# First token group of an mLSTM cell with a SwiGLU block: dense landing of k and q, 64-row turns, values in column halves, and another order of loads and weight conversion

## The chip, the core and the metric

The kernel runs on one core of a Trainium2 chip. The metric is the time of one execution on the device in microseconds (us), lower is better; the runs' median is compared. The engines are TensorE (PE, matrix products and transposes), VectorE (DVE), ScalarE (ACT, also table functions), GpSimd (POOL) and SyncE (SP, which here only asks for DMA transfers). Each engine runs its own instructions in program order and waits on semaphores for the others. On-chip memory has 128 partitions; matrix products write to PSUM banks.

## What is computed

The reference, cut to what matters (B=4, H=8, S=768, D=40; 3072 tokens, model width 320, hidden width 1536):

```python
for t in range(S):                                  # mLSTM cell, per batch and head
    m_new = max(f[t] + m, i[t])
    f_stab, i_stab = exp(f[t] + m - m_new), exp(i[t] - m_new)
    C = f_stab * C + i_stab * outer(v[t], k[t])
    n = f_stab * n + i_stab * k[t]
    y[t] = sigmoid(o[t]) * (C @ q[t]) / max(abs(n @ q[t]), 1.0)
x = y.transpose(0, 2, 1, 3).reshape(B * S, H * D)
out = (silu(x @ w_gate) * (x @ w_val)) @ w_out      # weights come as float64
```

## The kernel before

**Stages.** The sequence is cut into six groups of 128 tokens; each group has 4 batches x 128 tokens = 512 columns. Within a group the cell is computed with products over the 128 tokens and a carried state. Then comes the feed-forward block: twelve hidden blocks m of 128 features (`hidden(0, m)` in the first group) and the output product (`project_all`). Group 0 has a prologue of its own (L526 to L664), in which nothing of the feed-forward block can run yet. The order of instructions is written out by hand: the calls in the prologue, then for each hidden block m the lists `ahead` (which weight blocks are converted behind it) and `slots` (what else is emitted behind it, L978 onward).

**The prologue.** P is a pair of batches (16 heads), u one batch. Seven burn products (L521) start PE. The masked decay weights are summed in eight PSUM banks (wps: L532, L536, L541) and exponentiated by ACT (`first_exp`, L547) into W0, which lives in h_sb[:, 0:8]. k and q are transposed (`first_turn`, L561) from tiles in which each head has 64 columns, 40 of data and 24 of zeros; `first_scores` (L571) multiplies, DVE applies the weights (L575). `first_own(u)` (L582) multiplies W0 with the values, eight heads, 128x128 by 128x41. `first_x(u)` (L587 to L590) divides, `first_gate(P)` (L596) multiplies with the sigmoid of the output gate (`sig`, L515) and POOL repeats 64 columns as padding (L597). `first_seam(P)` (L616) transposes x into xT, and `first_state(P)` (L604) makes the carried state. The first `hidden` product, gv_ps (L706), needs xT of both pairs and the converted weights of block 0.

**Weights.** They come as 64-bit floats and are converted on the chip: `scale(j)` is two ACT products (L212, L214), `join(j)` two DVE instructions (L221, L222), `rounded(j)` one addition on DVE or POOL (L229). They are loaded in pieces (`piece_load`, L187): p0 and p1 hold one hidden block each (m = 0, 1), p2 to p6 two each (p2: m = 2, 3). A piece has a gate part (partitions 0 to 63, asked for by SP) and two value parts (partitions 64 to 127, asked for by ACT up to p4). p2 lands in h_sb[:, 1:6], which W0 occupies first, p3 in h_sb[:, 8:13], p4 in wo_sb, the others in two buffers of their own.

**Later gates.** f_sb and i_sb hold the gates of the later 640 tokens. Their sums (`late_sums`, L296 to L298) and running maxima (`late_maxima`, L301 to L303) are written to M_dram and read back as w_sb for group 1 (L484), which first goes into `add` (L379).

**hidden(0, m)** makes two products into two PSUM banks (four such banks rotate), then ACT takes silu of the first (L711) and DVE multiplies with the second (L712). Block m+2 therefore needs the banks that L711 and L712 of block m release.

Of the kernel before, what the change touches and what calls it, by code (L numbers as in the profile page):

```python
# [18 lines left out]
L = 128  # L19
# [5 lines left out]
def kernel(  # L25
# [47 lines left out]
    def flat(t):  # L73
        return t.rearrange("p c t -> p (c t)")

    def bank(name, tag="cell"):
        return psum.tile([128, 512], F32, name=name, tag=tag)
# [26 lines left out]
    def heads(P):  # L104
        return slice(P * UH, (P + 1) * UH)
# [31 lines left out]
    def load(dst, a, c, P):  # L137
        nc.sync.dma_start(out=dst[:, heads(P), 0:D], in_=tokens(a, c, P))

    def copy(eng, dst, src):  # L140
        if eng is nc.scalar:
            nc.scalar.copy(dst, src)
        else:
            eng.tensor_copy(dst, src)

    def gate_rows(a):
        return a.rearrange("b h s -> (b h) s")
# [3 lines left out]

    nc.scalar.dma_start(out=f0, in_=spread_rows(f_gate))
    nc.sync.dma_start(out=i0, in_=spread_rows(i_gate))
    nc.scalar.dma_start(out=flat(f_sb), in_=gate_rows(f_gate)[:, L:])
    nc.scalar.dma_start(out=flat(i_sb), in_=gate_rows(i_gate)[:, L:])


    raws = {}
    PIECES = [("gv", 0, 1), ("gv", 1, 1)] + [("gv", m, 2) for m in range(2, NFC, 2)] + [("o", m, 4) for m in range(0, NFC, 4)]

    def piece_load(p, home=None):
        kind, m, n = PIECES[p]
        if kind == "gv":
            a, d = NKC, n * 128
            gate_w, val_w = (w[:, m * 128:(m + n) * 128].rearrange("(c p) f -> p c f", p=HP) for w in (moe_w_gate, moe_w_val))
            src = [(slice(0, HP), slice(0, NKC), gate_w), (slice(HP, 128), slice(0, NKC - 1), val_w[:, 1:]),
                   (slice(HP, 128), slice(NKC - 1, NKC), val_w[:, 0:1])]
            queues = (nc.sync,) + 2 * (nc.scalar if p < 5 else nc.sync,)
        else:
            a, d = n, DM  # L170
            src = [(slice(0, 128), slice(0, n), moe_w_out[m * 128:(m + n) * 128].rearrange("(a p) d -> p a d", p=128))]
            queues = (nc.sync,)
        if src[0][2].dtype == F32:
            for r, cs, w in src:
                if kind == "o":
                    nc.sync.dma_start(out=wo_sb[r, m:m + n, :], in_=w)
                else:
                    for x in range(n):
                        nc.sync.dma_start(out=wgv_sb[r, m + x, cs], in_=w[:, :, ts(x, 128)])
            return  # L180
        if home is None:
            raw = conv.tile([128, 4 * NKC * 128], U32, name="raw")
        else:
            raw = home.rearrange("p a t -> p (a t)").bitcast(U32)
        raw = raw[:, 0:2 * a * d]
        for (r, cs, w), queue in zip(src, queues):
            queue.dma_start(out=raw[r].rearrange("p (a d) -> p a d", a=a)[:, cs], in_=w.bitcast(U32))  # L187
        words = raw.rearrange("p (a d two) -> p a d two", two=2, a=a)
        raws[p] = (words[:, :, :, 0], words[:, :, :, 1])
        split(p)  # L190
# [40 lines left out]
    def convert(j, eng=None):  # L231
        scale(j)
        join(j)
        rounded(j, eng)

    for P in range(2):
        load(k_sb, k, 0, P)
        load(q_sb, q, 0, P)
        load(v_sb, v, 0, P)
    load(o_sb, o_gate, 0, 0)  # L240


    junk = early.tile([128, 512], BF16)
# [51 lines left out]
    def late_sums():  # L295
        nc.vector.tensor_tensor_scan(flat(f_sb), flat(keep1), flat(f_sb), 0.0, op0=ALU.mult, op1=ALU.add)  # L296
        nc.gpsimd.memset(step1, 0.0)
        nc.gpsimd.tensor_sub(i_sb, i_sb, f_sb)  # L298
# [166 lines left out]
    def xT(n):  # L465
        return xT_sb
# [47 lines left out]
    def sig(P):  # L514
        nc.scalar.activation(o_sb[:, heads(P)], o_sb[:, heads(P)], AF.Sigmoid)  # L515


    def burn(n, tag="cell"):
        t = bank("burn", tag)
        for _ in range(n):  # L520
            nc.tensor.matmul(t, lhsT=junk[:, 0:128], rhs=junk, start=True, stop=True)  # L521
# [22 lines left out]
    def first_exp(P):  # L544
        for j in range(2):
            for u in (2 * P, 2 * P + 1):
                nc.scalar.activation(W0[:, u * H + j * HH:u * H + (j + 1) * HH], wps[u, j], AF.Exp)  # L547

    w_end = early.tile([128, BH, 1], F32)

    def first_values(P):
        nc.gpsimd.tensor_copy(w_end[:, heads(P)], W0[:, heads(P), end])
        nc.gpsimd.tensor_tensor(vw_sb[:, heads(P)], v_sb[:, heads(P)], w_end[:, heads(P)].to_broadcast([128, UH, D1]),
                                op=ALU.mult)

    def first_turn(P, src, dst, engs):
        for b in range(2):
            tp = bank("tp_kq").rearrange("p (a t) -> p a t", t=L)
            for a in range(UA // 2):
                h = P * UH + b * H + 2 * a  # L560
                nc.tensor.transpose(tp[:, a, :], src[:, h:h + 2, :].rearrange("p h d -> p (h d)"), ident)  # L561
            a = P * UA + b * UA // 2
            copy(engs[b], dst[:, a:a + UA // 2, :], tp)

    def first_scores(P):
        for b in range(2):
            sp = [bank("sp").rearrange("p (a t) -> p a t", t=L) for _ in range(2)]
            a0 = P * UA + b * UA // 2
            for a in range(UA // 2):
                for two in range(2):  # L570
                    nc.tensor.matmul(sp[two][:, a, :], lhsT=kT[half(two), a0 + a, :], rhs=qT[half(two), a0 + a, :],  # L571
                                     start=True, stop=True)
            W = W0[:, 2 * a0:2 * a0 + H].rearrange("p (a two) t -> p two a t", two=2)
            for two in range(2):
                nc.vector.tensor_tensor(W[:, two], sp[two], W[:, two], op=ALU.mult)  # L575
# [3 lines left out]
    def first_own(u):  # L579
        first_y[u] = bank("first_y", "gen")[:, 0:H * D1].rearrange("p (h d) -> p h d", d=D1)  # L580
        for h in range(H):
            nc.tensor.matmul(first_y[u][:, h, :], lhsT=W0[:, u * H + h, :], rhs=v_sb[:, u * H + h, :], start=True, stop=True)  # L582

    def first_x(u):
        y = first_y.pop(u)
# [4 lines left out]
        nc.vector.tensor_tensor(x_sb[:, u, 0:DM].rearrange("p (h d) -> p h d", d=D), y[:, :, 0:D],  # L590
                                den.to_broadcast([128, H, D]), op=ALU.mult)

    def first_gate(P):
        for u in (2 * P, 2 * P + 1):
            x = x_sb[:, u, 0:DM].rearrange("p (h d) -> p h d", d=D)
            nc.vector.tensor_tensor(x, x, o_sb[:, u * H:(u + 1) * H], op=ALU.mult)  # L596
        nc.gpsimd.tensor_copy(x_sb[:, 2 * P:2 * P + 2, DM:], x_sb[:, 2 * P:2 * P + 2, 0:HP])  # L597

    def first_state(P, tag="cell"):
        ps = small("add", tag=tag)  # L600
# [6 lines left out]
    def first_kept(P, ps, eng):  # L607
        copy(eng, state(2)[:, P * UA:(P + 1) * UA], ps)

    def first_seam(P, engs):  # L610
        for c, eng in zip(range(0, NKC, 2), engs):
            cs = range(c, min(c + 2, NKC))
            tp = bank("tp_x")[:, 0:len(cs) * 2 * L].rearrange("p (c u s) -> p c u s", u=2, s=L)
            for w in cs:
                for b in range(2):
                    nc.tensor.transpose(tp[:, w - c, b, :], x_sb[:, 2 * P + b, ds(w * HP, 2 * HP)], ident)  # L616
            copy(eng, xT(0)[:, c:c + len(cs), 2 * P * L:(2 * P + 2) * L].rearrange("p c (u s) -> p c u s", u=2), tp)

    burn(7)
    banks = [(u, j) for j in range(2) for u in range(B)]  # L620
    for f in (first_mask, first_inputs, first_maxima):
        for u, j in banks:
            f(u, j)
    first_exp(0)
    first_turn(0, k_sb, kT, (V, V))
    first_turn(0, q_sb, qT, (A, V))
    first_exp(1)
    first_values(0)
    first_scores(0)
    first_own(0)  # L630
    late_sums()
    first_turn(1, k_sb, kT, (A, A))
    first_x(0)
    first_turn(1, q_sb, qT, (A, V))
    load(o_sb, o_gate, 0, 1)
    piece_load(0)
    first_own(1)
    first_values(1)
    first_scores(1)
    first_x(1)  # L640
    sig(0)
    piece_load(1)
    burn(3)
    first_own(2)
    piece_load(2, h_sb[:, 1:1 + NKC])
    sig(1)
    burn(2)
    first_own(3)
    first_gate(0)
    first_x(2)  # L650
    first_x(3)
    first_gate(1)
    first_seam(0, (A, A, V))
    scale(0)
    ps1 = first_state(1, "gen")
    burn(1, "gen")
    piece_load(3, h_sb[:, NH - NKC:])
    join(0)
    first_seam(1, (A, A, V))
    rounded(0, V)  # L660
    first_kept(0, first_state(0), A)
    first_kept(1, ps1, V)
    convert(1, V)
    nc.scalar.activation(warm, warm, AF.Silu)  # L664
    piece_load(4, wo_sb)
    piece_load(5)


    pair = early.tile([BH, PP], F32)
# [289 lines left out]
    def load_all(dst, a, n):  # L959
        for P in range(2):  # L960
# [7 lines left out]
    ahead[0] = []  # L968
    ahead.update({4: [6], 5: [7, 8], 6: [9], 7: [10], 8: [11], 9: [], 10: [], 11: []})
    slots = {  # L970
        0: [run(convert, 2, V), run(late_maxima), run(load_all, k_sb, k, 1),
            run(nc.sync.dma_start, out=M_dram, in_=flat(M_sb)), run(load_all, q_sb, q, 1)],
        1: [run(piece_load, 6), run(late_decay)],
        2: [run(nc.scalar.activation, step1, step1, AF.Exp), run(decay_rows), run(weights_load, 1), run(load_all, v_sb, v, 1)],
        3: [run(late_turns)],
        4: [run(decay), run(cap_table)],
# [131 lines left out]
```

## Time and profile before

| what | us |
|---|---|
| median of 3 runs | 512.71 (512.23 to 512.75) |
| profiled execution, its own time | 513.3 |
| span in its trace | 511.5 |
| PE busy, share of the span | 505.1, 99% |
| end of the first pair's exponentials (ACT L547) | 11.61 |
| first scores product on PE (L571) | 12.52 |
| end of the last score product on DVE (L575) | 24.07 |
| end of the second gate (L596) | 28.96 |
| first gv_ps product (L706) | 31.92 |
| p2: parts asked for (ACT, SP, ACT) | 24.67, 24.92, 26.27 |
| p2: last part landed | 36.40 |
| scaling of block 2 on ACT (L212) | 36.98 |
| first gv_ps product of block 2 | about 40.66 |

Times in the trace run from the start of the span; the profiled execution is 1.8 us longer than its span. A timeline line reads: start, length, engine, line, operation, output<-inputs, shape, count, and in brackets the idle time before it with what ended it. "SPq" and "ACTq" lines are requests for transfers; the landing is a later event. In the DMA view, q1 is the queue that SP's requests go to and q10 that of ACT's.

### The profile page before, as it was taken

Reading aid. Unit: us, or ns where it says so; the run is one execution under the profiler, and the core shown is the slowest. Engines: PE = TensorE matmul, PEld = TensorE weight load, DVE = VectorE, ACT = ScalarE, POOL = GpSimd, SP = SyncE. Lnnn points to the kernel's source line nnn. Section 1 sums busy time; section 2 is a strip of 40 time slices with the busy share of each in tenths; the row PEclk is TensorE's granted clock in tenths of the full one; section 3 lists DMA queues with packets and bytes.
Section 4 is the critical chain, followed back from the end, with each engine's and each line's share of the span. In section 5 each row is a group of like instructions: output and inputs, shape, how many; then the busy total and the mean of one; then the engine's idle time right before and its main releaser. Section 6 shows DMA issues by size and latency. Waiting matters only on the chain.

```text
span 511.5 us, 14788 instructions
## 1 busy us (share of the span) xinstructions
PE 505.1 (99%) x6307; PEld 428.8 (84%) x6309; DVE 332.3 (65%) x539; ACT 204.8 (40%) x394; POOL 255.0 (50%) x274
## 2 busy tenths in 40 slices
PE   8999999999999999999999999999999999999997
PEld 4964445667888899988899888899988899988896
DVE  5779767887897777687466678467658554233421
ACT  3477655448512339312339321338421340223210
POOL 1303427475879663367652457652447650166710
PEclk9999999999999999999999999999999999999999
DMA  9999999698502992501993411993101200000001
GB/s 123 174 232 238 168 194 244 148 177 119 88 1 45 143 130 39 92 3 26 156 134 42 75 21 27 156 131 43 42 3 19 37 3 27 27 1 0 1 14 38
DMA packets 205497, 43.27 MB, mean 85 GB/s; under 512 B 193432, under 2 KB 200600, under 8 KB 205432
## 3 DMA queue, kind: packets, MB, share of 16 engines
q1 hardware_dynamic: 203444, 39.49, 49.4%
q10 hardware_dynamic: 1988, 2.85, 2.4%
q8 instruction: 49, 0.80, 0.7%
q14 instruction: 16, 0.13, 0.1%
HBM read 35.68 MB, written 4.01 MB: 78 GB/s over the span
## 4 chain that ended last, share of the span: by engine, by line
PE 91%; DMA 2%; DVE 2%; issue 1%; POOL 1%; ACT 1%; SPq 0%; DVEq 0%; ACTq 0%; POOLq 0%
PE gv_x L854 26%; PE o_ps L777 23%; PE gv_y L854 21%; PE gv_ps L706 5%; PE o_ps L723 5%; DMA w_sb<-M_dram 2%; PE inter L402 2%; PE intra L411 2%; PE sp L353 2%; PE first_y L582 1%; PE add L379 1%; POOL w_sb L493 1%; PE burn L521 1%; PE tp_kq L561 1%; PE sp L571 1%
## 5 line engine op out<-in xcount | busy, mean ns | idle before, releaser
L854 PE MATMUL gv_x<-xT,wgv_sb 64*128 64x256 f32 x720 | 89.1, 377 | 0.0
L854 PEld LDWEIGHTS gv_x<-xT,wgv_sb 64*128 64x128 f32 x720 | 69.6, 187 | 7.9 <-issue 0.2
L777 PE MATMUL o_ps<-wo_sb,h_sb 128*128 128x160 f32 x480 | 67.4, 300 | 0.0
L777 PEld LDWEIGHTS o_ps<-wo_sb,h_sb 128*128 128x128 f32 x480 | 65.6, 190 | 1.7 <-issue 1.7
L902 ACT ACTIVATE h_sb<-gv_x 128x256 f32<-128x256 f32 x30 | 11.5, 383 | 117.8 <-PE gv_x L854 117.8
L706 PE MATMUL gv_ps<-xT,wgv_sb 64*128 64x512 f32 x240 | 53.7, 596 | 0.3 <-DVE wgv_sb L229 0.3
L706 PEld LDWEIGHTS gv_ps<-xT,wgv_sb 64*128 64x128 f32 x240 | 23.6, 187 | 24.4 <-issue 23.2
L854 PE MATMUL gv_y<-q_sb,wgv_sb 64*128 64x256 f32 x360 | 44.0, 377 | 0.0
L854 PE MATMUL gv_y<-xT,wgv_sb 64*128 64x256 f32 x360 | 43.9, 376 | 0.0
L854 PEld LDWEIGHTS gv_y<-q_sb,wgv_sb 64*128 64x128 f32 x360 | 34.9, 187 | 4.2 <-DVE tmp L894 0.4
L854 PEld LDWEIGHTS gv_y<-xT,wgv_sb 64*128 64x128 f32 x360 | 35.0, 187 | 3.9
L364 POOL TENSOR_TENSOR vw_sb<-v_sb,w_sb 128x656 f32<-128x656 f32 x10 | 14.6, 1467 | 41.2 <-ACT w_sb L509 40.0
L777 PE MATMUL o_ps<-wT,S 128*128 128x160 f32 x240 | 33.4, 299 | 0.0
L777 PEld LDWEIGHTS o_ps<-wT,S 128*128 128x128 f32 x240 | 32.9, 190 | 0.0
L509 ACT ACTIVATE w_sb<-w_sb,g_T 128x64 f32<-128x64 f32 x128 | 31.0, 334 | 0.0
L854 PE MATMUL gv_x<-q_sb,sw 64*128 64x256 f32 x240 | 31.0, 376 | 0.0
L875 POOL TENSOR_TENSOR h_sb<-x_sb 128x512 f32<-128x512 f32 x12 | 15.8, 1314 | 24.6 <-ACT x_sb L874 24.6
L895 POOL TENSOR_TENSOR tmp<-tmp 128x512 f32<-128x512 f32 x15 | 20.0, 1332 | 14.5 <-DVE tmp L894 14.5
L875 POOL TENSOR_TENSOR h_sb<-tmp 128x512 f32<-128x512 f32 x13 | 16.5, 1269 | 21.5 <-ACT tmp L874 21.5
L744 POOL TENSOR_TENSOR S<-h_sb 128x256 f32<-128x256 f32 x30 | 22.6, 752 | 9.2 <-DVE h_sb L875 7.3
L854 PE MATMUL gv_y<-q_sb,sw 64*128 64x256 f32 x200 | 27.0, 388 | 0.0
L723 PE MATMUL o_ps<-wo_sb,h_sb 128*128 128x320 f32 x96 | 26.9, 437 | 0.0
(221 smaller groups left out, 984.6 us busy)
## 6 DMA issues: line engine op xcount, KB each, us to landing
w_sb<-M_dram SPq DMA_DIRECT2D x10, 512.0 KB, 7.1
k_sb<-in_k_dram SPq DMA_DIRECT2D x12, 320.0 KB, 7.4
v_sb<-in_v_dram SPq DMA_DIRECT2D x12, 320.0 KB, 5.5
o_sb<-in_o_gate_dram SPq DMA_DIRECT2D x12, 320.0 KB, 6.8
raw<-in_moe_w_out_dram SPq DMA_DIRECT2D x3, 1280.0 KB, 7.5
x_sq<-k_sb SPq DMA_DIRECT2D x64, 40.0 KB, 2.0
q_sb<-in_q_dram SPq DMA_DIRECT2D x32, 64.0 KB, 3.8
out_dram<-tmp SPq DMA_DIRECT2D x24, 80.0 KB, 1.7
```

Source lines behind the costliest of these rows:

```text
L353: nc.tensor.matmul(sp[two][half(i), a, :], lhsT=kT[feats(two), P * UA + a, half(i)], rhs=qT[feats(two), P * UA + a, half(i)], start=True, ...
L364: eng.tensor_tensor(vw_sb[:, heads(P)], v_sb[:, heads(P)], w_sb[:, heads(P), last].to_broadcast([128, UH, D1]), op=ALU.mult)
L402: nc.tensor.matmul(inter[two][half(i), a, :], lhsT=qT[feats(two), P * UA + a, half(i)], rhs=state(2 * n + i)[feats(two), P * UA + a, :], s ...
L509: nc.scalar.activation(w_sb[:, h], w_sb[:, h], AF.Exp, bias=g_T[:, n, h:h + 1], scale=-1.0)
L706: nc.tensor.matmul(ps[i], lhsT=wgv_sb[half(i), m, kc, :], rhs=x[half(i), kc, :], start=(kc == 0), stop=(kc == NKC - 1))
L723: nc.tensor.matmul(ps[u], lhsT=hid(g, m)[:, ts(u, L)], rhs=wo_sb[:, m, :], start=(m == 0), stop=(m == NFC - 1))
L744: eng.tensor_tensor(S1[:, k], lo[:, second_half], hi[:, second_half], op=ALU.add)
L777: nc.tensor.matmul(node[x][:, i], lhsT=lhs(k)[:, ts(i, L)], rhs=rhs(k), start=start and k == 0 and i == 0, stop=stop and k == KH - 1, skip ...
L854: nc.tensor.matmul(ps[:, i, cols], lhsT=lhs(c)[half(i)], rhs=rhs(c)[half(i)], start=start and c == 0, stop=stop and c == n - 1, skip_group ...
L875: (nc.vector if k == KH - 1 else nc.gpsimd).tensor_tensor(h_sb[:, 2 * k + 1], uw[:, 0], uw[:, 1], op=ALU.mult)
L895: nc.gpsimd.tensor_tensor(uw[:, :, second_half], uw[:, :, second_half], uw[:, :, first_half], op=ALU.add)
L902: nc.scalar.activation(h[:, first_half], x[:, 0, first_half], AF.Silu)
```

## The change

- k and q of the first group land dense (16 heads x 40 columns) in h_sb[:, 8:13], q first; DVE (q of pair 0) and POOL (the other three) copy them into the padded tiles. v follows.
- The requests for f_sb and i_sb move from ACT's start to SP, right behind p2's gate part.
- k and q are turned by `turn_one`, which transposes 64 rows at a time into two banks, and x by `seam`, likewise; `first_turn` and `first_seam` go.
- `first_own` is split into column halves: each head's product becomes two of 64 output rows.
- The prologue's order is written anew: own(0) and own(1) both come before scores(1), state(0) before own(3). Pair 0's gate and its padding are on POOL, pair 1's padding on ACT, rounding of block 0 on POOL. Three groups of burn products (3, 2 and 1) go.
- p1's value parts are asked for by POOL. p2 is asked for in two steps: the gate part and the first value part behind the second gate, the second value part behind the second seam's copies; the first value part stands on ACT behind the padding. SP's requests for p3's and p4's gate parts come directly behind the late gates; the value parts of p4 stand behind block 0's silu on ACT.
- The conversion of block 2 and the sums of the later gates come before hidden(0, 0) instead of behind it, so on ACT the scaling of block 2 precedes block 0's silu, and on DVE its joining, its rounding and the scan of the sums precede block 0's product. The running maxima, the M_dram write and the load of the next q come one block later.

`piece_load` gets an argument `parts` (which of the three transfers to ask for); the rest of it is unchanged.

```diff
@@ -151,39 +151,45 @@
 
     nc.scalar.dma_start(out=f0, in_=spread_rows(f_gate))
     nc.sync.dma_start(out=i0, in_=spread_rows(i_gate))
-    nc.scalar.dma_start(out=flat(f_sb), in_=gate_rows(f_gate)[:, L:])
-    nc.scalar.dma_start(out=flat(i_sb), in_=gate_rows(i_gate)[:, L:])
+
+    def late_gates():
+        nc.sync.dma_start(out=flat(f_sb), in_=gate_rows(f_gate)[:, L:])
+        nc.sync.dma_start(out=flat(i_sb), in_=gate_rows(i_gate)[:, L:])
...
+    homes = {}
+
-            queues = (nc.sync,) + 2 * (nc.scalar if p < 5 else nc.sync,)
+            queues = (nc.sync,) + 2 * (nc.gpsimd if p == 1 else nc.scalar if p < 5 else nc.sync,)
...
+        if p in homes:
+            raw = homes[p]
+        elif home is None:
             raw = conv.tile([128, 4 * NKC * 128], U32, name="raw")
         else:
             raw = home.rearrange("p a t -> p (a t)").bitcast(U32)
-        raw = raw[:, 0:2 * a * d]
-        for (r, cs, w), queue in zip(src, queues):
+        raw = homes[p] = raw[:, 0:2 * a * d]
+        for (r, cs, w), queue in [(src[x], queues[x]) for x in parts if x < len(src)]:
             queue.dma_start(out=raw[r].rearrange("p (a d) -> p a d", a=a)[:, cs], in_=w.bitcast(U32))
...
+    dense = h_sb[:, NH - NKC:].rearrange("p m t -> p (m t)").rearrange("p (x h d) -> p x h d", x=4, d=D)
+
+    def load_dense(x, a, P):
+        nc.sync.dma_start(out=dense[:, x], in_=tokens(a, 0, P))
+
+    def spread(eng, x, dst, P):
+        copy(eng, dst[:, heads(P), 0:D], dense[:, x])
+
     for P in range(2):
-        load(k_sb, k, 0, P)
-        load(q_sb, q, 0, P)
+        load_dense(2 * P, q, P)
+        load_dense(2 * P + 1, k, P)
+    for P in range(2):
         load(v_sb, v, 0, P)
-    load(o_sb, o_gate, 0, 0)
 
 
...
+    def first_ends(P):
+        nc.gpsimd.tensor_copy(w_end[:, heads(P)], W0[:, heads(P), end])
+
     def first_values(P):
-        nc.gpsimd.tensor_copy(w_end[:, heads(P)], W0[:, heads(P), end])
         nc.gpsimd.tensor_tensor(vw_sb[:, heads(P)], v_sb[:, heads(P)], w_end[:, heads(P)].to_broadcast([128, UH, D1]),
                                 op=ALU.mult)
-
-    def first_turn(P, src, dst, engs):
-        for b in range(2):
-            tp = bank("tp_kq").rearrange("p (a t) -> p a t", t=L)
-            for a in range(UA // 2):
-                h = P * UH + b * H + 2 * a
-                nc.tensor.transpose(tp[:, a, :], src[:, h:h + 2, :].rearrange("p h d -> p (h d)"), ident)
-            a = P * UA + b * UA // 2
-            copy(engs[b], dst[:, a:a + UA // 2, :], tp)
 
...
     def first_own(u):
         first_y[u] = bank("first_y", "gen")[:, 0:H * D1].rearrange("p (h d) -> p h d", d=D1)
         for h in range(H):
-            nc.tensor.matmul(first_y[u][:, h, :], lhsT=W0[:, u * H + h, :], rhs=v_sb[:, u * H + h, :], start=True, stop=True)
+            for i in range(2):
+                nc.tensor.matmul(first_y[u][half(i), h, :], lhsT=W0[:, u * H + h, half(i)], rhs=v_sb[:, u * H + h, :],
+                                 start=True, stop=True)
 
...
-    def first_gate(P):
-        for u in (2 * P, 2 * P + 1):
+    def first_gate(P, engs, pad):
+        for u, eng in zip((2 * P, 2 * P + 1), engs):
             x = x_sb[:, u, 0:DM].rearrange("p (h d) -> p h d", d=D)
-            nc.vector.tensor_tensor(x, x, o_sb[:, u * H:(u + 1) * H], op=ALU.mult)
-        nc.gpsimd.tensor_copy(x_sb[:, 2 * P:2 * P + 2, DM:], x_sb[:, 2 * P:2 * P + 2, 0:HP])
+            eng.tensor_tensor(x, x, o_sb[:, u * H:(u + 1) * H], op=ALU.mult)
+        copy(pad, x_sb[:, 2 * P:2 * P + 2, DM:], x_sb[:, 2 * P:2 * P + 2, 0:HP])
 
...
-    def first_seam(P, engs):
-        for c, eng in zip(range(0, NKC, 2), engs):
-            cs = range(c, min(c + 2, NKC))
-            tp = bank("tp_x")[:, 0:len(cs) * 2 * L].rearrange("p (c u s) -> p c u s", u=2, s=L)
-            for w in cs:
-                for b in range(2):
-                    nc.tensor.transpose(tp[:, w - c, b, :], x_sb[:, 2 * P + b, ds(w * HP, 2 * HP)], ident)
-            copy(eng, xT(0)[:, c:c + len(cs), 2 * P * L:(2 * P + 2) * L].rearrange("p c (u s) -> p c u s", u=2), tp)
-
+    spread(V, 0, q_sb, 0)
+    spread(G, 1, k_sb, 0)
     first_exp(0)
-    first_turn(0, k_sb, kT, (V, V))
-    first_turn(0, q_sb, qT, (A, V))
+    turn_one(0, q_sb, qT, (V, A))
+    turn_one(0, k_sb, kT, (V, A))
     first_exp(1)
+    first_ends(0)
+    spread(G, 2, q_sb, 1)
+    spread(G, 3, k_sb, 1)
+    first_scores(0)
+    turn_one(1, q_sb, qT, (A, A))
+    turn_one(1, k_sb, kT, (A, A))
     first_values(0)
-    first_scores(0)
+    piece_load(0)
+    load(o_sb, o_gate, 0, 0)
+    load(o_sb, o_gate, 0, 1)
     first_own(0)
+    first_ends(1)
+    first_values(1)
+    first_own(1)
+    first_x(0)
+    first_x(1)
+    first_scores(1)
+    sig(0)
+    first_gate(0, (G, G), G)
+    scale(0)
+    first_own(2)
+    first_x(2)
+    sig(1)
+    ps0 = first_state(0)
+    first_own(3)
+    piece_load(1)
+    seam(0, 0, (A, A, A, A))
+    first_x(3)
+    first_gate(1, (V, V), A)
+    join(0)
+    piece_load(2, h_sb[:, 1:1 + NKC], (0, 1))
+    rounded(0)
+    ps1 = first_state(1, "gen")
+    seam(0, 1, (A, V, A, A))
+    piece_load(2, parts=(2,))
+    late_gates()
+    scale(1)
+    first_kept(0, ps0, V)
+    join(1)
+    first_kept(1, ps1, A)
+    rounded(1, V)
+    piece_load(3, h_sb[:, NH - NKC:])
+    nc.scalar.activation(warm, warm, AF.Silu)
+    convert(2, V)
     late_sums()
-    first_turn(1, k_sb, kT, (A, A))
-    first_x(0)
-    first_turn(1, q_sb, qT, (A, V))
-    load(o_sb, o_gate, 0, 1)
-    piece_load(0)
-    first_own(1)
-    first_values(1)
-    first_scores(1)
-    first_x(1)
-    sig(0)
-    piece_load(1)
-    burn(3)
-    first_own(2)
-    piece_load(2, h_sb[:, 1:1 + NKC])
-    sig(1)
-    burn(2)
-    first_own(3)
-    first_gate(0)
-    first_x(2)
-    first_x(3)
-    first_gate(1)
-    first_seam(0, (A, A, V))
-    scale(0)
-    ps1 = first_state(1, "gen")
-    burn(1, "gen")
-    piece_load(3, h_sb[:, NH - NKC:])
-    join(0)
-    first_seam(1, (A, A, V))
-    rounded(0, V)
-    first_kept(0, first_state(0), A)
-    first_kept(1, ps1, V)
-    convert(1, V)
-    nc.scalar.activation(warm, warm, AF.Silu)
-    piece_load(4, wo_sb)
-    piece_load(5)
...
     slots = {
-        0: [run(convert, 2, V), run(late_maxima), run(load_all, k_sb, k, 1),
-            run(nc.sync.dma_start, out=M_dram, in_=flat(M_sb)), run(load_all, q_sb, q, 1)],
-        1: [run(piece_load, 6), run(late_decay)],
+        0: [run(piece_load, 4, wo_sb), run(piece_load, 5), run(load_all, k_sb, k, 1)],
+        1: [run(late_maxima), run(nc.sync.dma_start, out=M_dram, in_=flat(M_sb)), run(load_all, q_sb, q, 1),
+            run(piece_load, 6), run(late_decay)],
```

More of the change, by code (lines that the diff above doesn't have):

```diff
@@ L153, with piece_load @@
     nc.sync.dma_start(out=i0, in_=spread_rows(i_gate))
-    nc.scalar.dma_start(out=flat(f_sb), in_=gate_rows(f_gate)[:, L:])
-    nc.scalar.dma_start(out=flat(i_sb), in_=gate_rows(i_gate)[:, L:])
+    def late_gates():
+        nc.sync.dma_start(out=flat(f_sb), in_=gate_rows(f_gate)[:, L:])
+        nc.sync.dma_start(out=flat(i_sb), in_=gate_rows(i_gate)[:, L:])
     raws = {}
     PIECES = [("gv", 0, 1), ("gv", 1, 1)] + [("gv", m, 2) for m in range(2, NFC, 2)] + [("o", m, 4) for m in range(0, NFC, 4)]
-    def piece_load(p, home=None):
+    homes = {}
+    def piece_load(p, home=None, parts=(0, 1, 2)):
         kind, m, n = PIECES[p]
@@ L173, in piece_load @@
         if src[0][2].dtype == F32:
-            for r, cs, w in src:
+            for r, cs, w in [src[x] for x in parts if x < len(src)]:
                 if kind == "o":
@@ L180, in piece_load @@
             return
-        if home is None:
+        if p in homes:
+            raw = homes[p]
+        elif home is None:
             raw = conv.tile([128, 4 * NKC * 128], U32, name="raw")
```

## The prediction

> **What bounds the kernel now.** I read the page first. TensorE (PE) is busy 99% of the span at full clock, so only stretches in which PE waits, or does work that this change alters, can move the end.
>
> ```profile
> span 511.5 us, 14788 instructions
> ...
> PE 505.1 (99%) x6307; PEld 428.8 (84%) x6309; DVE 332.3 (65%) x539; ACT 204.8 (40%) x394; POOL 255.0 (50%) x274
> ...
> PEclk9999999999999999999999999999999999999999
> DMA  9999999698502992501993411993101200000001
> ```
>
> The first DMA digits are full: the first 40 us are also a queue of loads. Next the chain of work that ended last, over the first 120 us:
>
> ```profile
> 28.16 0.80 DVE x_sb L596 x2
> ...
> 30.96 0.82 DVE wgv_sb L229
> 31.79 0.14 issue
> 31.92 17.46 PE gv_ps L706 x80
> ...
> 84.44 0.94 DVE w_sb L360 x2
> 85.39 0.26 issue
> 85.64 1.28 DVE w_sb L360 x2
> 86.97 1.14 PE add L379 x62
> ```
>
> Column one is the start, column two the length. Up to 31.92 PE's work is scaffolding; from there PE runs gapless, 4.365 us (17.46/4) for each hidden block m. So **two instants matter**: when the first gv_ps matmul starts (31.92), and whether every later block's weights are in time. The chain names one later stall, at the first `add`, about 0.65 us of PE idle. It is fed by w_sb, which the DMA brought in (59.33 to 70.10 in the chain). How the prologue fills PE is in its timeline:
>
> ```profile
> 18.52 1.88 PE L582 MATMUL first_y<-v_sb,h_sb 128*128 128x41 f32 x16
> 20.32 2.06 PE L571 MATMUL sp<-qT,kT 64*128 64x128 f32 x32
> ...
> 26.82 1.29 PE L616 MATMUL tp_x<-ident,x_sb 128*128 128x128 f32 x10
> 28.04 1.13 PE L604 MATMUL add<-vw_sb,k_sb 128*64 128x41 f32 x32
> ```
>
> **Part 1, up to the first gv_ps matmul.** I lay out the new order with these durations.
> - Early loads. Six 160-byte loads follow each other at about 2 us (k 8.53, q 10.96, v 12.77, k 15.18 landed). Without f_sb and i_sb ahead (landed 8.66, 8.96) I take 0.8 us off (160 KB at some 200 GB/s). The o loads land dense in the kernel before and take the same 2 us, so I give dense landing nothing (bounds: 0 to 0.4 us a load). It adds four spreading copies; the nearest rows are 0.69 (a DVE copy of 512) and 1.29 (a POOL product of 656). They lie under the mask sums on PE (to 10.38) and ScalarE's (ACT's) exponentials (9.54 to 11.61).
> - q's turn, 0.50 us in 64-row form, runs at 10.4; k's waits for a PSUM bank that the last exponential frees, 11.65 to 12.15. Two copies side by side (0.69) give kT at 13.0: scores(0) start at 13.05 instead of 12.52, **+0.5**.
> - From there I add up. Score products on DVE end at 16.8. Each own(u) falls from 1.88 to 1.13 if 64 columns cost what L604's 64 columns cost: same 32 instructions, same 41 columns (bounds 1.13 and, if nothing is saved, 1.88). The sums' scan (1.47 at 16.19) and the late turn copy leave DVE. scores(1) start at 19.6 instead of 20.32, products end at 23.35 instead of 24.07: **-0.7**. Then own(2) to 23.3, state 24.4, own(3) to 25.55 instead of 27.00; x(3) (1.1) to 26.8; gate(1) (0.88) to 27.65 instead of 28.96: **-1.3**.
> - Padding goes to ACT (about 0.3, POOL's 0.29), the seam's 20 transposes take 0.77 (the later seam, L476) instead of 1.29, its copies end near 30.4. join(0) (0.49+0.82) stands directly behind the gate, to 29.0, without the seam copy in front (0.33). rounded(0) goes to POOL: 1.55 instead of 0.82, **+0.7**, to 30.6. First gv_ps at **30.65: gain 1.27** (0.5 to 1.7 by the bounds). The removed burns lie in PE waits and cost nothing while PE's pauses stay short.
>
> **Part 2, weights for block m=2.** These come from the third piece, p2: gate half on SP, value half in two DMAs on ACT. Two moves matter.
>
> (a) convert(2) and the scan of the sums now stand in front of m=0's silu and product on ACT and DVE. PE's m=2 needs the PSUM banks which these release. So everything waits for p2's landing X: scale 2x0.8, join 0.49+0.82, rounded 0.82, scan 1.47, then m=0's product 0.69. With overlaps as at 36.98 to 40.11 in the rows before, rounded ends at X+3.1, the scan at X+4.55, m=2 starts at **X+5.25**. PE itself is ready at 30.65+8.73 = 39.38, so no stall needs X below 34.1. Before, p2 landed at 36.40 and m=2 still started at 40.66, since silu and product did not stand behind it.
>
> (b) p2's value half is asked for later: before at 24.67 (512 KB, landed 31.81) and 26.27 (128 KB, landed 35.44). Now the first waits on ACT behind gate(1)'s padding, near 28.0, and the second behind the last seam copies, near 30.4. Meanwhile SP asks for p2's gate part at 23.5, then the late gates (160 KB) and the gate parts of p3 and p4 (640 KB each), near 25 instead of 28.91 and 29.55: their only waits are loads that landed by then. Whether those pass ahead of p2's value half is the dispute. Two windows of the DMA view bear on it. 30.95 to 32.65 us:
>
> ```profile
> q1 hardware_dynamic: 165, 0.34, 102.7%
> ```
>
> and 37 to 41 us:
>
> ```profile
> q1 hardware_dynamic: 347, 0.68, 55.0%
> q10 hardware_dynamic: 328, 0.61, 49.6%
> ```
>
> q1 is SP's queue, q10 ACT's. In the first window p2's last part, asked at 26.27, moves no packet while SP's load runs alone at 208 GB/s; in the second both move, 322 GB/s together. So a load sometimes waits for the other queue and sometimes shares.
>
> X by cases. p0's data end about 1 us earlier than before, at 24.3 instead of 25.29. p1 and p2's gate part (1.31 MB at 220 GB/s) then end at 30.25. If p2's first value part shares at once with gates and p3, 0.52 MB at half of 320 ends at 33.5, the second at 34.3, landing 1.65 later as before: X = **36.0**. If it enters only when p3's gate part is three quarters through (33.2), data end at 37.3: X = **38.9**. If p4 also goes ahead: data end 39.9, X = **41.5**. The lower end: p0's two value parts landed 4.05 and 5.10 after issue, so 30.4 gives **34.45 to 35.5**. I take **37.5**, midway between sharing and one load ahead, since the rows show both.
>
> m=2 then starts at 42.75 instead of 40.66: **+2.1**, a PE stall of 3.4 us that swallows Part 1's gain.
>
> The Trainium skill (SBUF — State Buffer, "Can I just issue two DMAs to hit both halves?") says that two loads at partition 0 and 64 together reach only 6% over one. This trace disagrees: 322 against 208 GB/s. By that rule alone sharing would save nothing and X would lie at the 38.9 end.
>
> **Part 3, after m=2.** From there PE's order is as before, shifted. late_maxima go one block later, the M_dram write near 47 instead of 51.29 (where SP stood 5.88 us in the k load), so w_sb comes some 4 us earlier and the 0.65 us at `add` should go: **-0.65**. p1's value half moves to POOL's queue, which no row of before shows: ACT's rows are 4.05 to 7.25 us, so it lands at 27.7 to 32; up to 31 costs nothing, and a delay of m=1 to 1 us would be absorbed in m=2's stall.
>
> **Sum.** +2.1 - 0.65 = +1.45 us. The profiled execution took 513.3 us (span 511.5 and 1.8 around it), so 514.75; the runs' median 512.71 lies 0.6 below that execution: **514.2 us**.
>
> **Rivals.**
> - A, p2 comes in time (faster). X = 34.1 to 35.5, since value packets sharing with SP's gain from 322 GB/s, or SP asks for p3 later than I think. For: the 4.05 and 5.10 us rows. Against: 7.15 and 9.17 us for this very piece. m=2 at 39.4 to 40.75: -1.3 to +0.1, less 0.65: 510.8 to 512.2; typical 511.2. It is the other side, and decides at X = 35.0.
> - B, fair sharing. X = 36.0, m=2 at 41.25, +0.6-0.65: 512.7, no change.
> - C, p4's gate part goes ahead too. X = 41.5, m=2 at 46.75, +6.1-0.65: 518.2. For: p4 is asked 3 us before the value half. Against: p4's value part, asked at 31.94, landed at 43.49, before its gate part (45.29), which was asked at 29.55.
> - D, the forecast's stall also cools PE's clock. The first seven burns took 0.45 us each (3.17/7) and the next eight, L532, 0.30, where 512 columns later cost 0.218 (17.46/80): a cold start costs 1.6+0.65 = 2.3. The rows before have no such gap after 1.19, so whether 3.4 us suffices is open: 516.5. The Trainium skill (TensorE: Matmul & The Clock Gate, "What's actually happening") gives one idle window of about 3.4 us for it; no run here shows that.
> - E, a part doesn't do what it says: own(u) not shorter in halves. Then own(2) and own(3) put gate(1) back by 1.5 (2 x 0.75), but while X sets m=2 this costs only as far as it delays p2's value half, 0 to 1.5: about +0.7, 514.9, inside the forecast.
>
> **Chances and range.** Forecast with E (X 36.7 to 39, 513.4 to 515.6) 0.36; A 0.32; B 0.16; C 0.09; D 0.07. A measurement of this kernel tells about 0.2% (1.0 us) from no change: faster 0.32, same 0.16, slower 0.52. The forecast's own range is 513.4 to 515.7. The 8-in-10 range takes in A, B and D and leaves out the top of C: 510.6 to 517.6.
>
> **What would show it.** Right: first gv_ps near 30.65; own(u) at 1.13; the scaling of block 2 on ACT ending a long wait for a DMA near 37.5; a PE gap ahead of the 41st gv_ps matmul with the DVE product as releaser; no idle at the first `add`. Wrong: p2 landed by 35, gv_ps gapless, then the time is A's; or the first gv_ps not before 31.9, in which case Part 1 fails and only the stall remains.

## The result, and the profile after

The changed kernel is slower: median 519.95 us (519.21 to 523.2, six runs) against 513.11 us of the kernel before in the same session, ratio 1.0135 with the 95% interval 1.0103 to 1.0168. The range on record ended at 517.6. The profiled execution took 523.2 us, the longest of the six, with a span of 521.4 us. Its page:

```profile
span 521.4 us, 15024 instructions
...
PE 507.6 (97%) x6419; PEld 424.9 (81%) x6419; DVE 331.3 (64%) x534; ACT 205.9 (39%) x400; POOL 260.7 (50%) x281
...
PEclk9987999999989999999999999999999999999999
```

PE is busy 2.5 us more than before although its work has not grown (the products are the same, some cut in halves, and six burn products are gone), and its clock is below full in slices 3, 4 and 12 (13 us each). The timeline of PE shows the prologue's products and the hidden blocks:

```profile
18.10 2.07 PE L590 MATMUL first_y<-v_sb,h_sb 128*64 128x41 f32 x64
20.10 2.06 PE L578 MATMUL sp<-qT,kT 64*128 64x128 f32 x32
...
24.48 1.11 PE L590 MATMUL first_y<-v_sb,h_sb 128*64 128x41 f32 x32
25.52 0.77 PE L490 MATMUL tp_x<-ident,x_sb 64*128 64x64 f32 x17
...
30.57 10.47 PE L714 MATMUL gv_ps<-xT,wgv_sb 64*128 64x512 f32 x40 [0.36 <-POOL wgv_sb L235]
43.65 1.60 PE L714 MATMUL gv_ps<-xT,wgv_sb 64*128 64x512 f32 x2 [2.62 <-DVE wgv_sb L235]
45.53 11.51 PE L714 MATMUL gv_ps<-xT,wgv_sb 64*128 64x512 f32 x38 [0.27 <-DVE h_sb L720]
```

Each own takes 1.1 us (two of them 2.07) instead of 1.88. The first gv_ps starts at 30.57, 1.35 earlier than before. Blocks 0 and 1 then take 10.47 instead of 8.73, there is a pause, and blocks 2 and 3 take 11.51 for 38 products, where 8.3 is usual. What the pause waited for is in the chain of waits:

```profile
30.30 9.96 DMA h_sb<-in_moe_w_val_dram
...
40.37 0.79 ACT top L218
...
42.68 0.10 DVE wgv_sb L235
...
43.42 1.47 DVE f_sb L310
44.89 0.59 DVE h_sb L720
```

p2's last value part, asked for at 30.30, landed at 40.27; behind it come the scaling, the rounding, the scan of the sums and block 0's product. (Two products of block 2 ran at 43.65, as soon as the weights were rounded; the next needed the bank that block 0's product frees.) The slow stretches are the clock, as PE's granted clock in stretches of the span shows (columns: stretch, its length, PE busy and instructions, clock, DMA share, GB/s; 1.00 is full clock):

```profile
26.00:30.00 4.00, 2.51 (x64) 1.00 1.01 239
30.00:34.00 4.00, 3.64 (x11) 0.57 1.07 208
34.00:41.00 7.00, 7.00 (x34) 1.00 1.04 312
41.00:45.00 4.00, 1.38 (x4) 0.89 1.07 228
45.00:51.00 6.00, 5.73 (x15) 0.51 1.20 175
```

Half clock from 30.4 to 33.9 and from 44.1 to 50.9. PE's instants put the two profiles side by side:

| PE reaches | before | after | difference |
|---|---|---|---|
| first gv_ps | 31.92 | 30.57 | -1.35 |
| end of block 3 (tp_g) | 49.31 | 56.97 | +7.66 |
| add of group 1 | 85.27 | 92.93 | +7.66 |
| end of the first output product | 125.75 | 131.94 | +6.19 |
| next add | 204.22 | 214.07 | +9.85 |
| last o_ps product | 507.83 | 517.68 | +9.85 |

Between the first two rows PE loses 9.0 us: 4.05 waiting for block 2 (from 41.04 to 45.53, less two products of 0.22) and the rest at half clock (1.7 in blocks 0 and 1, 3.2 in blocks 2 and 3). Up to 131.94, 1.5 us come back, 0.8 of them at the first `add`, where PE no longer waits. The last 3.7 are a third place, in group 1:

```profile
PE gv_x L862 <- DVE C L409: 2.3, 1, 2.3
```

This is one wait of 2.3 us, followed by half clock. The other five runs are 2.2 to 4 us shorter than the profiled one; whether they lack this third loss is not known, since only one execution was profiled.

### The profile page after: what moved, and what is told of

The parts are those of the page before. It is cut to its first block, busy times and chain, and to the rows that moved or that the text cites. A ratio compares the mean times of both kernels' runs of the same rounds, so it can differ in the third digit from the quotient of the medians.

```text
span 521.4 us, 15024 instructions
## 1 busy us (share of the span) xinstructions
PE 507.6 (97%) x6419; PEld 424.9 (81%) x6419; DVE 331.3 (64%) x534; ACT 205.9 (39%) x400; POOL 260.7 (50%) x281
## 4 chain that ended last, share of the span: by engine, by line
PE 86%; DMA 3%; SPq 2%; DVE 2%; issue 1%; POOL 0%; ACT 0%; DVEq 0%; ACTq 0%
PE gv_x L862 24%; PE o_ps L785 22%; PE gv_y L862 20%; PE gv_ps L714 9%; PE o_ps L731 3%; PE inter L416 2%; PE sp L367 2%; DMA h_sb<-in_moe_w_val_dram 2%; SPq L351 2%; PE intra L425 2%; PE add L393 1%; DMA raw<-in_k_dram 1%; DVE C L409 1%; POOL wo_sb L235 0%; PE tp_kq L332 0%
## 5 line engine op out<-in xcount | busy, mean ns | idle before, releaser
L714 PE MATMUL gv_ps<-xT,wgv_sb 64*128 64x512 f32 x240 | 59.7, 638 | 3.2 <-DVE wgv_sb L235 2.6
```

The lines of the kernel that those rows point to most:

```text
L714: nc.tensor.matmul(ps[i], lhsT=wgv_sb[half(i), m, kc, :], rhs=x[half(i), kc, :], start=(kc == 0), stop=(kc == NKC - 1))
```

## The experiments

Theory Q: requests to the DMA are served in the order in which they were asked for, whichever queue takes them; p2's value half therefore stands behind p3's and p4's gate parts, and block 2 starts 5.25 us behind its landing. Rival S: the DMA engines are full, whoever asks first. Rival K: the loss is the clock, which the removed burn products kept up. A later theory, L, says where an early gain is lost again. All ratios are against the kernel before in the same session, with their 95% intervals; that kernel's median was 514.36, 512.53 and 514.86 in the three sessions, so ratios are compared, not times.

**1. Conversion of block 2 behind block 0 again** (changed kernel).

```diff
-    convert(2, V)
-    late_sums()
...
-        0: [run(piece_load, 4, wo_sb),
+        0: [run(convert, 2, V), run(late_sums), run(piece_load, 4, wo_sb),
```

> The changed kernel with the conversion of block 2 and the sums of the later gates emitted behind hidden(0, 0) again. Theory Q (requests are served in the order in which they were asked, so p2's value half waits behind p3's and p4's gate parts, and everything that block 2 needs follows p2's landing): p2 still lands near 40.3, block 0's silu and product no longer stand behind it, the second product of block 2 needs only the rounded weights, so block 2 starts at 43.65 and goes on at once instead of at 45.53: 1.9 us less, near 518.0; if PE's pause of 2.6 us is then too short for the second stretch at half clock, 2.8 less still, near 515.2. Rival K (the loss is the halved clock that came with the removed burn products, not the landing): first half-clock stretch at 30.4 to 33.8 stays and the time changes by less than 0.7.

Measured 517.31, ratio 1.0068 (1.0038 to 1.0099): half of the loss goes. p2 landed at 40.03 and block 2 went on from 43.33 without the second wait:

```profile
43.33 4.56 PE L712 MATMUL gv_ps<-xT,wgv_sb 64*128 64x512 f32 x20 [1.20 <-DVE wgv_sb L235]
```

The pause was 1.2 us (blocks 0 and 1 had run 6 us at half clock), and the clock stayed full from 43 to 51. So the place of the conversion cost about 2 us directly (45.53 against 43.33), and the clock that fell behind the longer pause came on top.

**2. SP asks for p2's value parts** (changed kernel).

```diff
-            queues = (nc.sync,) + 2 * (nc.gpsimd if p == 1 else nc.scalar if p < 5 else nc.sync,)
+            queues = (nc.sync,) + 2 * (nc.gpsimd if p == 1 else nc.scalar if p < 5 and p != 2 else nc.sync,)
...
-    piece_load(2, h_sb[:, 1:1 + NKC], (0, 1))
+    piece_load(2, h_sb[:, 1:1 + NKC])
...
-    piece_load(2, parts=(2,))
```

> The changed kernel, but SP asks for p2's value parts right behind p2's gate part (near 24.5 and 25.1), ahead of the later gates and of p3's and p4's gate parts. Theory Q: p2's data end near 33 and it lands near 34.2 instead of 40.27; block 2 follows block 1 without a gap (near 41.0, since blocks 0 and 1 still run partly at half clock); no second stretch at half clock: 4.5 + 2.8 us less, near 512.7, level with the kernel before. Rival S (the 16 DMA engines are simply full, whoever asks first): p2 lands at 37 or later and less than half of that is gained, 516 or more. Rival K: 518 or more.

Measured 515.08, ratio 1.0014 (0.9996 to 1.0032). Asked for at 23.62, the large value part landed at 32.54, and all four blocks follow each other:

```profile
29.75 20.33 PE L713 MATMUL gv_ps<-xT,wgv_sb 64*128 64x512 f32 x80 [0.48 <-POOL wgv_sb L235]
```

Rival S falls: the same bytes over the same engines, only asked for in another order, and nine tenths of the loss go. The 20.33 us, where 17.46 are usual, are half clock again (0.50 in 30 to 34).

**3. ACT asks for p2's value parts early** (changed kernel: both behind own(2), ahead of the scaling of block 0).

```diff
     first_gate(0, (G, G), G)
-    scale(0)
     first_own(2)
     first_x(2)
+    piece_load(1)
+    piece_load(2, h_sb[:, 1:1 + NKC])
+    scale(0)
...
-    piece_load(1)
...
-    piece_load(2, h_sb[:, 1:1 + NKC], (0, 1))
...
-    piece_load(2, parts=(2,))
```

> The changed kernel, but ACT asks for both of p2's value parts behind own(2) (near 23.8 and 24.5), ahead of the scaling of block 0, instead of near 27.6 and 30.3. Theory Q, in which only the time of asking counts and not the queue: p2 lands near 34.2, as if SP asked, and the time is 512.7 within 1 us. Rival: ACT's queue as such is served behind SP's: p2 lands after 37 and the time is 515 or more. Rival K: 518 or more.

Measured 514.53, ratio 1.0019 (0.9986 to 1.0052), the same as with SP. In the DMA view of 22.0 to 22.8 us the large value part lands 5.6 us after it was asked for, ahead of SP's gate part:

```profile
h_sb<-in_moe_w_gate_dram SPq DMA_DIRECT2D x1, 640.0 KB, 10.4
h_sb<-in_moe_w_val_dram ACTq DMA_DIRECT2D x1, 512.0 KB, 5.6
```

So here the time of asking counts, not which of the two queues takes the request.

**4. Burn products back** (changed kernel, 3, 2 and 1).

```diff
     scale(0)
+    burn(3)
     first_own(2)
...
     ps0 = first_state(0)
+    burn(2)
     first_own(3)
...
     ps1 = first_state(1, "gen")
+    burn(1, "gen")
```

> The changed kernel with the burn products of the kernel before put back: 3 ahead of own(2), 2 ahead of own(3), 1 behind state(1). Rival K: both stretches at half clock go, 1.7 + 2.8 us less, near 515.5. Theory Q: the clock at the first hidden block may stay full and blocks 0 and 1 end near 39.4 instead of 41.0, but block 2 still starts 5.25 us behind p2's landing near 40.3, after a longer pause, at half clock: 519.9 within 0.8.

Measured 520.94, ratio 1.0138 (1.0092 to 1.0184): nothing gained, so K falls as the first cause. The clock stays full through blocks 0 and 1, and the time goes into the wait:

```profile
31.09 8.85 PE L717 MATMUL gv_ps<-xT,wgv_sb 64*128 64x512 f32 x40
44.12 12.32 PE L717 MATMUL gv_ps<-xT,wgv_sb 64*128 64x512 f32 x39 [4.18 <-DVE wgv_sb L235]
```

Blocks 0 and 1 are done at 39.9, p2 lands at 40.67, and the pause brings half clock for the blocks behind it.

**5. Both repairs**: experiment 2 with the burn products of experiment 4.

> Both repairs together: SP asks for p2's value parts right behind p2's gate part, and the burn products are back (3, 2 and 1). With the landing out of the way the clock should count. Theory Q with the clock as a second cause: no stretch at half clock at the first hidden blocks (28 to 35 us there without the burns, some 2.8 us of PE), first gv_ps near 30.3, blocks 0 to 3 end near 47.8 instead of 49.38, and the 0.65 us at add gone: about 2 us less than the kernel before, ratio 0.996, and 2.5 less than with the value parts alone. Rival (the clock matters little; the early gain is given back elsewhere): the same as with the value parts alone, ratio 1.001.

Measured 513.75, ratio 1.0017 (0.9998 to 1.0037): missed, no better than without burns. The clock is full and the four blocks take 17.44 us, but the burns stand on the path: own(3) starts at 25.46 instead of 24.48 in the changed kernel, the first gv_ps at 31.57 instead of 30.57. Block 3 ends 0.4 ahead of the kernel before, and that is lost later.

**6. The kernel before without its three later groups of burn products.**

```diff
-    burn(3)
...
-    burn(2)
...
-    burn(1, "gen")
```

> The kernel before with its three later groups of burn products (3, 2 and 1) taken out and nothing else. If the burns are what keeps the clock full up to the first gv_ps: a stretch at half clock from about 30 to 34 and 1.7 us more or, with its whole window in hidden blocks, up to 3; ratio 1.003 to 1.006. If it is the change's shorter products and pauses (halves, 64-row turns) that let the clock fall: clock 1.0 up to the end and ratio 1.000.

Measured 516.87, ratio 1.0065 (1.0044 to 1.0087). Half clock, at the prologue's products:

```profile
24.00:27.00 3.00, 3.00 (x27) 0.89 1.14 218
27.00:30.00 3.00, 3.00 (x35) 0.54 1.10 211
```

The first gv_ps is 2.8 late, at 34.68. So six products that compute nothing are worth about 0.6% there. In the changed kernel they show no worth: with p2 late PE waits for it anyway (experiment 4), and with p2 in time the full clock that they bring is paid for by the later start (experiments 2 and 5, ratios 1.0014 and 1.0017).

**7. Values in whole columns** (both repairs, `first_own` as before).

```diff
-            for i in range(2):
-                nc.tensor.matmul(first_y[u][half(i), h, :], lhsT=W0[:, u * H + h, half(i)], rhs=v_sb[:, u * H + h, :],
-                                 start=True, stop=True)
+            nc.tensor.matmul(first_y[u][:, h, :], lhsT=W0[:, u * H + h, :], rhs=v_sb[:, u * H + h, :], start=True, stop=True)
```

> Both repairs, but first_own in whole columns as in the kernel before (one product of 128 output rows for each head instead of two of 64). If the halves are worth what the rows say (1.13 instead of 1.88 for each own): own(2) and own(3) are on the path, first gv_ps 1.5 us later, near 31.8, ratio 1.5 us (0.003) above that of both repairs. If PE waits for DVE there anyway: first gv_ps within 0.4 and no difference.

Measured 520.93, ratio 1.0139 (1.0096 to 1.0181), first gv_ps at 37.20: far more than expected. All four own products are on the path, since own(0) and own(1) now stand ahead of the second scores (by the durations 4 x 0.75 = 3.0 us, not 1.5), and half clock fell on 19.0 to 25.8, some 3.4 us. The first is what the halves should be worth in this order; the second may be the lot of this kernel's pauses, and no run separates the two.

**8. Padded landing of k and q** (both repairs, no spreading copies).

```diff
-        load_dense(2 * P, q, P)
-        load_dense(2 * P + 1, k, P)
+        load(q_sb, q, 0, P)
+        load(k_sb, k, 0, P)
```

> Both repairs, but k and q land straight in the padded tiles again, in the new order (q, k, q, k), without the spreading copies. Dense loads followed each other by about 1.7 us, padded ones by 2 to 2.4: the fourth load lands near 14 instead of 11.7 and the last v near 19 instead of 16.4. If the start is bound by the exponentials up to 12.1 and by DVE behind them: first gv_ps within 0.5 us of that with dense landing, ratio within 0.001. If the later loads (values, weights of block 0) are bound by this queue: first gv_ps 1 us or more later.

Measured 520.2, ratio 1.0129 (1.0095 to 1.0163): also far more. The first four landings are 7.55, 9.97, 12.37, 14.68 instead of 6.32, 8.13, 9.93, 11.73: 2.4 us a load against 1.8. Everything behind them is late, up to p1's small value part (37.02 instead of 31.26), for which block 1 waits until 40.38, and the clock is at half from 27.8 to 38.

**9, 10, 11. The small loads of k first.** In the profile of experiment 2 PE waits 2.82 us in group 1, at the place of the third loss:

```profile
136.07 1.13 PE L861 MATMUL gv_x<-xT,wgv_sb 64*128 64x256 f32 x8 [2.82 <-DVE C L409]
```

C waits for DVE's transposes of k, and these for the last of sixteen small loads, which SP asks for behind the next o load. The last landed 1.6 us after SP had issued it in the kernel before (127.76), 3.3 in the changed one (136.51). So (9: both repairs, 10: the kernel before, 11: experiment 2):

```diff
-        3: [run(do_divide, 1, 1), run(load_all, o_sb, o_gate, 2), run(early_squares, 0), run(weights_cap, 0)],
+        3: [run(do_divide, 1, 1), run(early_squares, 0), run(load_all, o_sb, o_gate, 2), run(weights_cap, 0)],
```

> Both repairs (SP asks for p2's value parts, burn products back), and in the first output product the sixteen small loads of k for group 2 are asked for ahead of the next o load instead of behind it. Theory L (the early gain is given back at the first gv_x of group 1, where PE waits for the state C, DVE's transposes of k and the last of these small loads: C ends 9.15 us behind the last o_ps product there, 8.5 in the kernel before, and PE arrives 8.8 behind it): DVE transposes k near 124 to 125 instead of 128.4, no PE idle there, 0.4 to 0.8 us less than both repairs alone and less spread: ratio 0.998 to 1.000. Rival (that place costs nothing): 1.0017 as before.

> The kernel before with that one exchange. Theory L: where the last small load lands early (1.6 us behind its request) nothing is gained, where it lands late (3.5 us) the 2.2 us of PE idle go: lowest time unchanged, near 511.9, the upper half of the runs (513.5 to 516) moves down, median 0 to 1 us less. Rival: no change of the spread.

> SP asks for p2's value parts, no burn products, and the exchange. Theory L: that profile's 2.75 us of PE idle at 132 to 136 go, so 1 to 2.7 us less than without the exchange: ratio 0.996 to 1.000, with the spread that the half-clock stretches leave. Rival: 1.0014 as before.

Measured 513.45, 513.54 and 513.34: ratios 0.9964 (0.9932 to 0.9996), 0.9967 (0.9934 to 1.0001) and 0.9964 (0.993 to 0.9997). The wait of DVE goes, here in kernel 9 (before it was 3.54 and ended at 127.98):

```profile
126.53 2.37 DVE L357 STREAM_TRANSPOSE kT<-raw 128x1024 f32<-128x1024 f32 x2 [0.69 <-issue]
```

Theory L holds for experiment 2's wait: in the profile of kernel 11 PE no longer waits for C. But the kernel before seems to gain as much from it (its interval just reaches 1; its runs without the exchange spread from 511.66 to 519.63 in that session), and the three do not differ: no gain of the new prologue can be seen. Kernel 11 starts its first gv_ps at 30.35 and ends block 3 at 49.22, against 49.31 before: half clock took the lead.

**12. Experiment 2 with the conversion of block 2 behind block 0.**

> SP asks for p2's value parts, and the conversion of block 2 and the sums stand behind hidden(0, 0) again. If the order of the conversion costs only because p2 lands late: the same as with the value parts alone, ratio 1.001 within 0.002. If it costs by itself: 1 to 2 us less, 0.997 to 0.999.

Measured 516.75, ratio 1.0039 (1.0004 to 1.0075): not better, if anything above both expected values, though the interval overlaps that of experiment 2. So with p2 in time there is no sign that the conversion ahead of block 0 costs anything. Why this kernel is not level with experiment 2 is open; in its profile PE waits 0.66 us for block 3's rounding and 1.1 at an o_ps product, which that of experiment 2 does not have.

## Why the prediction was wrong

- **The first gv_ps** was forecast at 30.65 and came at 30.57. The steps held too: the second scores were 0.5 late (20.10 against 19.6), from own(3) on all were within 0.2. Two sizes were off without effect on it: dense landing, to which I gave nothing, is worth 0.6 us a load (experiment 8), and rival E's 1.5 for the halves counted own(2) and own(3) alone.
- **X, p2's landing, is the first step that failed.** The form X+5.25 held to 0.01 us (40.27 + 5.25 = 45.52; measured 45.53). X itself was put at 37.5, midway between sharing and one load ahead. It was 40.27: the large value part, asked for at 27.60, moved its first packet at 34.34, when p3's gate part was out and p4's under way. That lies between my 38.9 and C's 41.5. The DMA view from 31 to 34 us has SP's queue alone:

```profile
q1 hardware_dynamic: 303, 0.59, 106.0%
```

and from 34.3 to 38 us both:

```profile
q1 hardware_dynamic: 288, 0.56, 53.3%
q10 hardware_dynamic: 284, 0.55, 51.1%
```

Experiments 2 and 3 show what decides: the time of asking. But Q in its strict form, one request after the other, does not hold. The value part, on an empty queue, did not move until the gate parts asked for before it had started; then the two queues shared, and it went beside p4's gate part, which landed at 39.64. In the kernel before, with both queues moving, p4's value part (asked for at 31.94) even landed ahead of its gate part (29.55). I read the two windows of the kernel before as waiting at times and sharing at times, and took the middle. The first is the case that counted: there p2's last part (26.27), on an empty queue, stood behind p2's own gate part (24.92). In the second both queues were already moving. Why an empty queue waits so is not shown. The term: +2.1 forecast, +4.9 measured.
- **The clock is the second.** I gave it 0.07 and let it stand alone, as rival D; it came together with the late landing. Its price was too low (2.3 forecast, 3.2 measured in blocks 2 and 3), and the sum of both, 514.2 + 2.8 + 2.3 to 3.2, lay outside the range. "The removed burns cost nothing" failed as a mechanism: without them a half-clock stretch came ahead of block 2, 1.7 us, which cost nothing only because p2 was later. In the kernel before the same removal costs 0.65% (experiment 6).
- **The 0.65 us at add** went, but by luck. The forecast was an earlier M_dram write, near 47, and w_sb 4 us earlier. The write was asked for at 51.38 (51.29 before), and the last of w_sb landed at 71.28 (72.66 before). PE simply came 7.7 us later. Where it came in time, in experiments 3 and 11, it waited at `add` again, here in 3:

```profile
86.08 2.33 PE L393 MATMUL add<-vw_sb,k_sb 64*64 64x41 f32 x126 [0.29 <-DVE w_sb L374]
```

- **What I did not see**: the wait in group 1, which was within 0.3 us of the path before (C ready at 134.33, PE there at 134.61) and turns a changed rhythm of the loads into 0 to 2.8 us.

The Trainium skill (TensorE: Matmul & The Clock Gate, "What's actually happening") gives two states, full and half, chosen by how busy PE was in windows of about 3.4 us. The trace agrees on the states and the windows. Half-microsecond stretches of the changed kernel catch the four edges:

```profile
30.00:30.50 0.50, 0.21 (x3) 0.94 1.26 289
33.50:34.00 0.50, 0.50 (x2) 0.64 1.07 197
44.00:44.50 0.50, 0.50 (x2) 0.60 1.05 197
50.50:51.00 0.50, 0.50 (x4) 0.57 1.54 130
```

Read as shares of full and half they lie at 30.44, 33.86, 44.10 and 50.93, which is 3.42, 3 x 3.41 and 2 x 3.41 apart: a fixed grid. So it was wrong to ask whether one pause reaches 3.4 us. The pauses ahead of 30.44 were below 0.8 us each, together 1.5 in 4. Where the grid falls differs from profile to profile (half clock begins at 29.51 in experiment 1, at 28.79 in 2), so the price of a pause can differ too: the 2.3 us in group 1 of the changed kernel lay within one window (139.67 to 143.09) and brought half clock behind it, while the 2.82 us of experiment 2 lay across an edge at 134.60 and brought none.

What makes a window count as idle stays open; it is not PE's idle time as the profile shows it. In experiment 7, PE stood idle for 1.81 us between 138.44 and 141.85, and the clock stayed full. In experiment 6 half clock began at 26.36, and the window ahead of it, with nothing but the small own products of 41 columns, was nearly all busy (columns as above):

```profile
22.95:26.36 3.41, 3.29 (x30) 1.00 1.17 214
```

So the burns may have worked as large products among small ones and not only as fillers of pauses; no run separates the two. Five profiles without burns fell at the first hidden block (the changed kernel and 1, 2, 11, 12), the one of experiment 3 did not; with burns 4, 5 and 9 did not, 8 did, and 7 fell earlier, at 19.0.

## What to carry to other kernels

A load that the next stage needs should be asked for ahead of the loads that it does not need; asked for early, it did as well on ACT as on SP here. Freeing a later request from its waits can put it in front. Look up what stands in front of a request when it is issued, not only its size and its rate. Before calling filler work on TensorE free to remove, price a window at half clock (1.7 us here) behind each stretch of pauses and small products that it broke up, and add that price to a forecast stall of some length: stalls of 2.6 and 4.2 us brought two such windows each, one of 1.2 us (experiment 1) none. And look for the next wait that is nearly on the path: here an early gain of 1.3 us had 0.3 us of room later on.

## What was not expected of the hardware

- Dense rows (16 heads x 160 bytes side by side in a partition) landed every 1.8 us, rows spread over 256-byte slots every 2.4 us, with the same packets of 160 bytes.
- A request's first packet came 6.7 us after it was issued (27.60 to 34.34) although its own queue was empty.
- A stretch of 4 us in which PE worked only 1.4 us (41 to 45) was followed by 6.8 us at half clock.
